# Fourier mixing with a gated convolution: the last 64 rows of two batches put into one tile of the last product

## The chip, the cores and the metric

The kernel runs on one core of a Trainium2 chip. The metric is the device time of one execution in microseconds (us). A difference of 2% or more would be called faster or slower.

## The reference, cut to what matters

```python
def _attn_ref(x):                       # x: 8 batches, 3136 rows, 256 features, fp32
    X = np.fft.fft(x, axis=1)
    X = np.fft.fft(X, axis=2)
    return X.real.astype(np.float32)

def _moe_ref(x, w_in, conv_w, w_out):   # w_in 256x1024, conv_w 3x1024, w_out 1024x256
    h = np.maximum(x @ w_in, 0.0)
    ...                                 # conv_out: three taps along the rows, zero at the ends of a batch
    gate = 1.0 / (1.0 + np.exp(-conv_out))
    return (h * gate @ w_out).astype(np.float32)
```

The real part of the transform is even in the rows, so the kernel computes half the rows and mirrors them. What matters here is the last product, `(h * gate) @ w_out`: its rows are cut into tiles of at most 128, and 3136 is 24.5 times 128.

## The kernel before

The kernel is one loop of 256 steps: 8 batches, 4 chunks of rows each, 8 blocks of 128 hidden features each. The stages of a step are spread over several turns of the loop, so that all engines work at once:

```python
    for t in range(n + LAG):            # LAG = 3
        ...
        sigmoid(steps[t - 2])           # ScalarE
        products(steps[t + 1])          # TensorE: pb and pa, the two halves of x @ w_in
        copies(steps[t + 1])            # ScalarE: nb
        combine(steps[t])               # VectorE: h, reads pa in PSUM and nb in SBUF
        run("dve")                      # VectorE: input folding or transform of a later batch
        first_tap(steps[t])             # ScalarE
        other_taps(steps[t - 1])        # VectorE: two taps
        gate(steps[t - 2])              # VectorE one half, GpSimd the other
        mm2(steps[t - LAG])             # TensorE: the last product
        run("pe")                       # TensorE: transform of the next batch
```

("..." marks cuts; conditions on `t` are left out.) A batch has 6, 6, 6 and 7 tiles in its four chunks. The seventh tile of the last chunk has 65 rows. Eight feature blocks times eight batches make 64 products of seven tiles. The gate is a multiplication of two tensors, cut in the middle:

```python
        m = n // 2
        gt(g[:, m:n], g[:, m:n], h[:, m + 1:n + 1], op=ALU.mult)     # GpSimd
        vt(g[:, 0:m], g[:, 0:m], h[:, 1:m + 1], op=ALU.mult)         # VectorE
```

The copies of finished tiles use three buffers of two tiles; a chunk of seven tiles needs four.

## Time and profile before

| | before |
|---|---|
| time, median of 3 runs | 1308.8 us (1307.44 to 1309.79) |
| span of the profiled execution | 1303.7 us |
| TensorE busy | 1203.4 us, 92% |
| VectorE busy | 1190.7 us, 91% |
| products of seven tiles | 64 |

Of the groups of instructions by shape, three (columns: line, engine, operation, output from inputs, shape, count, then busy us, mean ns of one, and idle time before them):

```profile
L514 POOL TENSOR_TENSOR g<-g,h 128x417 f32<-128x417 f32 x64 | 62.0, 969 | 217.4 <-ACT g L507 92.6 <-DVE h L492 58.8 <-issue 34.2
...
L174 DVE TENSOR_TENSOR w<-xh 99x508 f32<-99x508 f32 x16 | 16.6, 1040 | 0.0
...
L175 DVE TENSOR_TENSOR w<-xh 99x508 f32<-99x508 f32 x16 | 10.8, 676 | 0.0
```

L174 and L175 fold the input of a later batch on VectorE. They have the same shape and the same number of elements, one adds and one subtracts, and yet one takes 1040 ns and the other 676. L514 is GpSimd's half of the gate of a last chunk. The timeline of a step in the stretch of batch 3 shows how they stand to each other (columns: start us, duration us, engine, line, operation, then the wait before it in brackets):

```profile
695.22 0.59 DVE L515 TENSOR_TENSOR g<-g,h 128x416 f32<-128x416 f32 x1
...
695.72 1.09 DVE L492 CUSTOM_DVE_ANT_0 h<-pa,nb 128x418 f32<-128x418 f32 x2
...
696.37 0.92 POOL L514 TENSOR_TENSOR g<-g,h 128x417 f32<-128x417 f32 x1 [3.71 <-ACT g L507]
696.72 1.11 DVE L174 TENSOR_TENSOR w<-xh 99x508 f32<-99x508 f32 x1
...
697.75 0.67 DVE L175 TENSOR_TENSOR w<-xh 99x508 f32<-99x508 f32 x1
```

L492, which reads PSUM, runs beside GpSimd's half and takes its usual time (two instructions in 1.09 us; over the whole trace, those of 417 columns take 583 ns on average where they overlap GpSimd's half, 57 of them, and 582 where they do not, 7 of them). L174, which reads two tensors in SBUF, begins beside it at 696.72 and takes 1.11 us. L175, begun after GpSimd is done, takes 0.67. So 0.44 us of L174's "busy" time look like time in which VectorE does not advance.

### The profile page before, as it was taken

The numbers are of one execution on the slowest core, as the hardware profiler recorded it, in microseconds if no ns is written. First come the engines' busy times: TensorE is split into PE (matmuls) and PEld (weight loads), VectorE is DVE, ScalarE is ACT, GpSimd is POOL, SyncE is SP. The second block draws the span as 40 slices with busy tenths as digits, with TensorE's granted clock in tenths as the row PEclk, the third lists the DMA queues.
The fourth block names the chain that finished last, engine by engine and source line by source line (L and its number), as shares of the span: only waits on it lengthen the run. The fifth ranks groups of instructions, "written<-read, shape, count | busy, mean of one in ns | idle before, by whom it ended". The sixth has DMA issues, their size and how long they took to land.

```text
span 1303.7 us, 15202 instructions
## 1 busy us (share of the span) xinstructions
PE 1203.4 (92%) x4914; PEld 898.9 (69%) x4914; DVE 1190.7 (91%) x1664; ACT 857.4 (66%) x1558; POOL 406.7 (31%) x507
## 2 busy tenths in 40 slices
PE   0758999999999999999899999999999999999998
PEld 0525677777677766777677776777677777777776
DVE  6869999999999998999899998999989888898996
ACT  0226676666667666677667776766767777777885
POOL 2415434241523234232513225241322223122222
PEclk9968999999999999999999999999999999999999
DMA  7601203020211112020202103020010001000011
GB/s 227 185 25 45 80 25 99 1 77 25 88 36 49 49 29 74 25 77 25 72 29 62 39 25 94 30 76 1 25 50 25 27 25 42 20 14 27 25 33 43
DMA packets 46841, 66.02 MB, mean 51 GB/s; under 512 B 5601, under 2 KB 35197, under 8 KB 46505
## 3 DMA queue, kind: packets, MB, share of 16 engines
q1 hardware_dynamic: 41012, 49.80, 12.1%
q0 software_dynamic: 5120, 12.85, 3.4%
q10 hardware_dynamic: 628, 2.40, 0.6%
q8 instruction: 38, 0.62, 0.2%
q14 instruction: 43, 0.34, 0.1%
HBM read 39.24 MB, written 25.74 MB: 50 GB/s over the span
## 4 chain that ended last, share of the span: by engine, by line
PE 57%; DVE 26%; issue 8%; ACT 4%; POOL 2%; DMA 2%; DVEq 0%; POOLq 0%; ACTq 0%; SPq 0%
PE po L89 36%; PE pb L89 8%; DVE g L504 7%; PE pa L89 7%; PE pd L89 6%; DVE h L492 4%; DVE g L515 4%; ACT nb L481 2%; DVE w L174 2%; DVE w L175 1%; DVE xh L158 1%; DVE xh L147 1%; DVE xh L163 1%; POOL er L319 1%; DVE xh L162 1%
## 5 line engine op out<-in xcount | busy, mean ns | idle before, releaser
L89 PE MATMUL po<-wout,g 128*128 128x256 f32 (+2 forms) x3200 | 744.9, 383 | 37.4 <-DVE g L515 22.0
L89 PEld LDWEIGHTS po<-wout,g 128*128 128x128 f32 (+2 forms) x3200 | 598.6, 189 | 206.0 <-DVE g L515 59.2
L504 DVE SCALAR_TENSOR_TENSOR g<-h,cw,g 128x770 f32<-128x770 f32 (+2 forms) x512 | 579.9, 1133 | 10.9 <-ACT g L498 1.8
L514 POOL TENSOR_TENSOR g<-g,h 128x385 f32<-128x385 f32 (+1 forms) x256 | 240.5, 941 | 775.4 <-ACT g L507 434.7
L507 ACT ACTIVATE g<-g 128x770 f32<-128x770 f32 (+2 forms) x256 | 220.6, 862 | 253.3 <-DVE g L504 252.2
L481 ACT ACTIVATE nb<-pb 128x386 f32<-128x386 f32 (+4 forms) x512 | 225.8, 494 | 95.7 <-PE pb L89 94.0
L492 DVE CUSTOM_DVE_ANT_0 h<-pa,nb 128x386 f32<-128x386 f32 (+4 forms) x512 | 265.1, 559 | 14.6 <-PE pa L89 9.6
L498 ACT ACTIVATE g<-h,cw 128x770 f32<-128x770 f32 (+2 forms) x256 | 243.8, 952 | 0.7 <-DVE h L492 0.7
L89 PE MATMUL pa<-pt,G 128*128 128x386 f32 (+2 forms) x512 | 213.6, 498 | 9.1 <-ACT pa L466 9.1
L89 PE MATMUL pb<-qt,G 127*128 127x386 f32 (+2 forms) x512 | 215.7, 502 | 4.5 <-ACT nb L481 4.5
L466 ACT ACTIVATE pa<-eb,ge 128x386 f32<-128x386 f32 (+2 forms) x256 | 154.0, 602 | 8.1 <-DMA eb<-ed 8.1
L515 DVE TENSOR_TENSOR g<-g,h 128x385 f32<-128x385 f32 (+2 forms) x256 | 153.0, 598 | 4.2 <-ACT g L507 4.2
L89 PEld LDWEIGHTS pa<-pt,G 128*128 128x128 f32 x512 | 97.5, 191 | 83.6 <-issue 21.0
L89 PE MATMUL pd<-tab,w 99*128 99x196 f32 (+2 forms) x448 | 119.0, 375 | 0.0
L89 PEld LDWEIGHTS pb<-qt,G 127*128 127x128 f32 x512 | 94.3, 191 | 31.8 <-ACT nb L481 7.7
L122 POOL DMA_INDIRECT xh<-in_x_dram,idx x64 | 88.8, 1388 | 16.4 <-issue 12.8
L89 PEld LDWEIGHTS pd<-tab,w 99*128 99x128 f32 (+1 forms) x448 | 83.7, 191 | 13.7
L531 ACT COPY os<-po 128x256 f32<-128x256 f32 (+2 forms) x200 | 59.8, 393 | 17.1 <-DMA out_dram<-os 9.6
L158 DVE TENSOR_TENSOR xh<-xh 98x1024 f32<-98x1024 f32 (+1 forms) x32 | 46.6, 1460 | 0.1
L147 DVE TENSOR_TENSOR xh<-xh 98x1020 f32<-98x1020 f32 (+1 forms) x32 | 45.6, 1435 | 0.0
L89 PE MATMUL po<-win,dm 128*128 128x512 f32 x8 | 5.7, 879 | 38.4 <-DMA dm<-dft_dim_dram 38.4
L174 DVE TENSOR_TENSOR w<-xh 98x508 f32<-98x508 f32 (+1 forms) x32 | 31.1, 971 | 0.1
(84 smaller groups left out, 350.8 us busy)
## 6 DMA issues: line engine op xcount, KB each, us to landing
out_dram<-os SPq DMA_DIRECT2D x184, 128.0 KB
xh<-in_x_dram SPq DMA_DIRECT2D x16, 784.0 KB
eb<-ed SPq DMA_DIRECT2D x16, 193.0 KB
tab<-dft_seq_dram SPq DMA_DIRECT2D x4, 601.8 KB
raw<-in_moe_w_in_dram ACTq DMA_DIRECT2D x2, 1024.0 KB
raw<-in_moe_w_out_dram SPq DMA_DIRECT2D x1, 2048.0 KB
eb<-ed SPq DMA_DIRECT2D x8, 209.0 KB
eb<-ed SPq DMA_DIRECT2D x8, 192.5 KB
```

Of the source, the lines that this page charges most:

```text
L89: nc.tensor.matmul(o, l, r, start=start, stop=stop, skip_group_check=True)
L122: nc.gpsimd.indirect_dma_start(out=xh[b, h][0:NP, 4 + m].rearrange("p q d -> p (q d)"), out_offset=None, in_=bass.AP(tensor=x.tensor, offs ...
L158: vt(flat(to, to + 2), flat(0, 2), flat(2, 4), op=op)
L466: act(pa[s][:, 0:n], eb[b, c], AF.Copy, scale=ge[:, f:f + 1])
L481: act(nb[s][:, i, cols], p[:, cols], AF.Copy, scale=-1.0 if i else 1.0)
L492: nc.vector._custom_dve(TENSOR_ADD_SAT, out=to, in0=a[:, cols], in1=c[:, i, cols], s0=BIG, s1=0.0)
L498: act(gs[s], hs[s][:, 0:n], AF.Copy, scale=cw[:, 0, s[2]:s[2] + 1])
L504: stt(out=g, in0=h[:, k:k + n], scalar=cw[:, k, f:f + 1], in1=g, op0=ALU.mult, op1=ALU.add)
L507: act(gs[s], gs[s], AF.Sigmoid)
L514: gt(g[:, m:n], g[:, m:n], h[:, m + 1:n + 1], op=ALU.mult)
L515: vt(g[:, 0:m], g[:, 0:m], h[:, 1:m + 1], op=ALU.mult)
L531: nc.scalar.copy(out=osb[0:m, j % 2], in_=pt[0:m, j % 2])
```

## The change

Its intent is to stop spending a whole tile on 65 rows. The limits of the chunks are moved so that every tile has 128 rows and 64 rows are left over per batch. The left-over rows of an even and an odd batch share one tile, `left`, which stays in SBUF and is multiplied with the odd batch. So the last chunk of an even batch has six tiles, and that of an odd batch has seven. VectorE writes the left-over columns with a multiply of its own, 64 wide, and the gate of a last chunk is split into 384 and 384 columns in place of 416 and 417. The core of the diff (moves of buffers and the arithmetic of the chunk limits are cut):

```diff
+    left = const.tile([P, NF, P], F32, name="left")
 ...
     def gate(s):
+        b, c, f = s
         g, h = gs[s], hs.pop(s)
         n = g.shape[1]
+        if chunks[c].last:
+            o = chunks[c].rest[0]
+            vt(left[:, f, b % 2 * LEFT:(b % 2 + 1) * LEFT], g[:, o:n], h[:, o + 1:n + 1], op=ALU.mult)
+            n = o
         m = n // 2
 ...
     def mm2(s):
-        tiles = chunks[c].tiles
-        for i, (o, r, m) in enumerate(tiles):
+        ch = chunks[c]
+        tiles = [(gs[s][:, o:o + m], [(0, b, r, m)]) for o, r, m in ch.tiles]
+        if ch.last and b % 2:
+            tiles.append((left[:, f], [(i * LEFT, b - 1 + i, ch.rest[1], LEFT) for i in range(2)]))
+        for i, (w, to) in enumerate(tiles):
 ...
-                    nc.sync.dma_start(out=rows[b * S + r:b * S + r + m, :], in_=osb[0:m, j % 2])
+                    for p0, b_, r, m in tiles[j][1]:
+                        nc.sync.dma_start(out=rows[b_ * S + r:b_ * S + r + m, :], in_=osb[p0:p0 + m, j % 2])
```

Besides, to make room for `left`, the pool of transform copies becomes four equal buffers, and the pool of broadcasts loses one of its five; the fourth broadcast of a batch is loaded later.

More of the change, by code (lines that the diff above doesn't have):

```diff
@@ L69 @@
     erp = ctx.enter_context(tc.tile_pool(name="erp", bufs=1))
-    ebp = ctx.enter_context(tc.tile_pool(name="ebp", bufs=5))
-    asp = ctx.enter_context(tc.tile_pool(name="asp", bufs=2))
+    ebp = ctx.enter_context(tc.tile_pool(name="ebp", bufs=4))
+    asp = ctx.enter_context(tc.tile_pool(name="asp", bufs=4))
     pqp = ctx.enter_context(tc.tile_pool(name="pqp", bufs=2))
@@ L252, in copy @@
             def copy(p):
-                a_[sn, c] = asp.tile([P, HO], F32, name="as", tag="as")
+                a_[sn, c] = asp.tile([P, HO + 2], F32, name="as", tag="as")
                 nc.scalar.copy(out=a_[sn, c][:, 0:n], in_=p[:, 0:n])
@@ L271, in copy @@
             def copy(p):
-                a_[sn] = asp.tile([P, HO + QO], F32, name="as", tag="ao")
-                nc.scalar.copy(out=a_[sn][:, HO:], in_=p[:, 0:QO])
+                a_[sn], a_["e0"] = [asp.tile([P, HO + 2], F32, name="as", tag="as") for _ in range(2)]
+                nc.scalar.copy(out=a_["e0"][:, 0:QO], in_=p[:, 0:QO])
             def fin(p):
-                a, e0, e2 = a_[sn], a_[sn][:, HO:], p[:, QO:2 * QO]
+                a, e0, e2 = a_[sn], a_["e0"][:, 0:QO], p[:, QO:2 * QO]
                 vt(a[:, 0:QO], e0, e2, op=ALU.add)
@@ L305, in copy @@
             def copy(p):
-                a_["e"] = asp.tile([P, HO + QO], F32, name="as", tag="ao"), asp.tile([P, HO], F32, name="as", tag="as")
+                a_["e"] = [asp.tile([P, HO + 2], F32, name="as", tag="as") for _ in range(2)]
                 for c in range(2):
@@ L330, in units, with spread @@
         return begin, [odd_even(1), odd(1), even(1, 0), even(1, 1), feature(), odd_even(0), odd(0), even(0, 0), even(0, 1)], row
-    def spread(b):
-        for c, ch in enumerate(chunks):
+    def spread(b, cs):
+        for c in cs:
+            ch = chunks[c]
             eb[b, c] = ebp.tile([P, HN], F32, name="eb", tag="eb")[:, 0:ch.k1 - ch.k0]
@@ L344, in __init__ @@
             c0 = CUTS[c]
-            c1 = CUTS[c + 1] if c + 1 < len(CUTS) else NK
-            self.k0, self.k1 = max(c0 - 1, 0), min(c1 + 1, NK)
+            self.last = c + 1 == len(CUTS)
+            c1 = NK - 1 if self.last else CUTS[c + 1]
+            self.k0, self.k1 = max(c0 - 1, 0), min(c1 + 2, NK)
             n = self.k1 - self.k0
-            f0 = 1 if c0 == 0 else 0
-            self.front = slice(f0, f0 + n)
-            b0, b1 = (1 if c0 == 0 else 0), (n - 1 if c1 == NK else n)
-            self.cols = slice(b0, b1)
-            self.back = slice(f0 + n, f0 + n + b1 - b0)
-            self.zeros = c0 == 0
-            self.w = self.back.stop + (1 if c0 == 0 else 0)
-            if c1 == NK:
-                runs = [(0, c0, S - 2 * c0 + 1)]
-            else:
-                runs = [(0, c0, c1 - c0), (f0 + n, S - c1 + 1, c1 - max(c0, 1))]
-            self.tiles = [(g + i, r + i, min(P, l - i)) for g, r, l in runs for i in range(0, l, P)]
+            self.zeros = c0 == 0
+            f0 = 1 if self.zeros else 0
+            nf = c1 + 1 - self.k0
+            b0, b1 = max(c0, 1) - self.k0, n - 1 if self.last else n
+            self.fcols, self.cols = slice(0, nf), slice(b0, b1)
+            self.front = slice(f0, f0 + nf)
+            self.back = slice(f0 + nf, f0 + nf + b1 - b0)
+            self.w = self.back.stop + f0
+            if self.last:
+                runs = [(0, c0, S - 2 * c0)]
+            else:
+                runs = [(0, c0, c1 - c0), (f0 + nf, S - c1, c1 - c0)]
+            self.tiles = [(g + i, r + i, P) for g, r, l in runs for i in range(0, l - LEFT, P)]
+            self.rest = (runs[0][2] - LEFT, runs[0][1] + runs[0][2] - LEFT)
+    LEFT = P // 2
+    assert B % 2 == 0 and all(c % P == 0 for c in CUTS) and (S - 2 * CUTS[-1]) % P == LEFT
     chunks = [Chunk(c) for c in range(len(CUTS))]
@@ L479, in copies @@
         nb[s] = nbp.tile([P, 2, HN], F32, name="nb", tag="nb")
-        for i, cols in enumerate((slice(0, n), ch.cols)):
+        for i, cols in enumerate((ch.fcols, ch.cols)):
             act(nb[s][:, i, cols], p[:, cols], AF.Copy, scale=-1.0 if i else 1.0)
@@ L490, in combine @@
             nc.gpsimd.memset(h[:, 0:ch.w:ch.w - 1], 0.0)
-        for i, (to, cols) in enumerate(((h[:, ch.front], slice(0, n)), (h[:, ch.back][:, ::-1], ch.cols))):
+        for i, (to, cols) in enumerate(((h[:, ch.front], ch.fcols), (h[:, ch.back][:, ::-1], ch.cols))):
             nc.vector._custom_dve(TENSOR_ADD_SAT, out=to, in0=a[:, cols], in1=c[:, i, cols],
@@ L518, in mm2 @@
         b, c, f = s
-        tiles = chunks[c].tiles
-        for i, (o, r, m) in enumerate(tiles):
+        ch = chunks[c]
+        tiles = [(gs[s][:, o:o + m], [(0, b, r, m)]) for o, r, m in ch.tiles]
+        if ch.last and b % 2:
+            tiles.append((left[:, f], [(i * LEFT, b - 1 + i, ch.rest[1], LEFT) for i in range(2)]))
+        for i, (w, to) in enumerate(tiles):
             if f == 0 and i % 2 == 0:
@@ L523, in mm2 @@
             pt = po[b, c, i // 2]
-            mm(pt[0:m, i % 2, :], gs[s][:, o:o + m], wout[:, f, :],
-               f == 0 and i % 2 == 0, f == NF - 1)
+            mm(pt[:, i % 2, :], w, wout[:, f, :], f == 0 and i % 2 == 0, f == NF - 1)
             if f == NF - 1 and (i % 2 or i == len(tiles) - 1):
@@ L529, in mm2 @@
                 for j in range(i - i % 2, i + 1):
-                    _, r, m = tiles[j]
-                    nc.scalar.copy(out=osb[0:m, j % 2], in_=pt[0:m, j % 2])
-                    nc.sync.dma_start(out=rows[b * S + r:b * S + r + m, :], in_=osb[0:m, j % 2])
+                    nc.scalar.copy(out=osb[:, j % 2], in_=pt[:, j % 2])
+                    for p0, b_, r, m in tiles[j][1]:
+                        nc.sync.dma_start(out=rows[b_ * S + r:b_ * S + r + m, :], in_=osb[p0:p0 + m, j % 2])
         gs.pop(s)
@@ L549 @@
         if i == 4:
-            spread(0)
+            spread(0, range(len(chunks)))
         for g in late_w[i::len(us)]:
@@ L591 @@
             at(cs[i + 1], "dve", u.fin)
-        at(cs[-1] - 2, "load", lambda b=b: spread(b))
+        at(cs[-1] - 2, "load", lambda b=b: spread(b, range(len(chunks) - 1)))
+        at(per * b + 1, "load", lambda b=b: spread(b, [len(chunks) - 1]))
     LAG = 3
```

## The prediction

> **What bounds the kernel now.** I first read the busy shares of the page.
>
> ```profile
> PE 1203.4 (92%) x4914; PEld 898.9 (69%) x4914; DVE 1190.7 (91%) x1664; ACT 857.4 (66%) x1558; POOL 406.7 (31%) x507
> ```
>
> TensorE and VectorE are one per cent apart over 1303.7 us, so work taken from one alone need not show in the time. Next come the groups by shape (busy us, mean ns, idle before).
>
> ```profile
> L89 PE MATMUL po<-wout,g 128*128 128x256 f32 x2944 | 690.3, 383 | 37.4 <-DVE g L515 22.0 <-POOL g L514 14.9
> L492 DVE CUSTOM_DVE_ANT_0 h<-pa,nb 128x386 f32<-128x386 f32 x256 | 130.5, 552 | 5.0 <-POOL g L514 5.0
> L89 PE MATMUL po<-wout,g 128*65 128x256 f32 x128 | 38.1, 379 | 0.0
> L492 DVE CUSTOM_DVE_ANT_0 h<-pa,nb 128x418 f32<-128x418 f32 x64 | 37.5, 586 | 0.0
> ```
>
> A tile of 65 rows costs what one of 128 costs (379 against 383 ns), so the last tile of each batch is half wasted: this is what the change goes for. But the same product waits 22.0 us for VectorE's half of the gate (L515).
>
> The question is which engine rules where the seventh tile stands. Steps run (batch, chunk, feature block); the loop does the last product three steps late, so the eight products of seven tiles fall at chunk 3, blocks 4 to 7 of the current step and chunk 0, blocks 0 to 3 of the next batch. I cut these stretches out of the trace for batches 0 to 6 (columns: us, then busy us and instructions of each engine).
>
> ```profile
> core 0: us, PE busy (x) PEld busy (x) DVE busy (x) ACT busy (x) POOL busy (x), PEclk, DMA share, GB/s
> 223.14:257.13 33.99, 32.45 (x131) 23.56 (x131) 32.69 (x43) 22.22 (x38) 7.70 (x11) 1.00 0.09 29
> 684.59:717.79 33.20, 32.20 (x132) 23.63 (x132) 32.46 (x44) 22.66 (x40) 12.50 (x17) 1.00 0.20 61
> 838.01:871.22 33.21, 32.19 (x132) 23.63 (x132) 32.47 (x44) 22.66 (x40) 12.49 (x17) 1.00 0.20 61
> 1138.78:1170.17 31.39, 31.39 (x131) 23.87 (x131) 29.85 (x42) 23.86 (x41) 7.66 (x11) 1.00 0.08 26
> ```
>
> In batches 0, 3 and 4 VectorE is busy longer than TensorE in just these stretches, because it folds the input of a later batch there; only in batch 6, where no fold is left, is TensorE full (31.39 of 31.39) and VectorE not. The timeline of batch 4's stretch (start, duration, instructions merged, wait in brackets) shows how:
>
> ```profile
> 853.89 0.59 DVE L515 TENSOR_TENSOR g<-g,h 128x416 f32<-128x416 f32 x1
> 854.53 3.29 PE L89 MATMUL po<-wout,g 128*128 128x256 f32 x14 [0.55 <-DVE g L515]
> ...
> 863.13 0.59 DVE L515 TENSOR_TENSOR g<-g,h 128x416 f32<-128x416 f32 x1
> 863.77 3.29 PE L89 MATMUL po<-wout,g 128*128 128x256 f32 x14 [0.34 <-DVE g L515]
> ```
>
> TensorE's product begins the moment VectorE's gate ends. A shorter product would only wait longer.
>
> Last, the end of batch 6's stretch:
>
> ```profile
> 1171.47 3.18 PE L89 MATMUL po<-wout,g 128*128 128x256 f32 x14
> 1175.79 2.75 PE L89 MATMUL po<-wout,g 128*128 128x256 f32 x12
> 1177.74 0.37 ACT L531 COPY os<-po 65x256 f32<-65x256 f32 x1 [2.83 <-DMA out_dram<-os]
> 1178.89 0.56 DVE L515 TENSOR_TENSOR g<-g,h 128x384 f32<-128x384 f32 x1 [3.05 <-ACT g L507]
> 1179.66 0.91 PE L89 MATMUL pb<-qt,G 127*128 127x385 f32 x2 [1.12 <-ACT nb L481]
> ```
>
> The copy of the seventh tile needs a fourth output buffer of three, waits 2.83 us for an output to land, and holds up ScalarE, then VectorE 3.05 and TensorE 1.12 us.
>
> [...]the 14 matmul instructions of seven tiles take 3.18 us and the 12 of six 2.75, so a tile costs 0.43 us[...]the trace has 551 ns for the 384-wide gate[...].
>
> **The change, part by part.**
>
> *Removed from TensorE.* In batches 0, 2, 4, 6 the eight last-chunk products go from seven tiles to six: 32 x 0.43 = 13.8 us, 1.05% of the time. The odd batches keep seven, the last of them the shared one.
>
> *Added to VectorE.* Each last-chunk step gets a 64-wide multiply into the shared tile, 64 in all; its own gate shrinks from 416 to 384 columns. A column costs (586-552)/32 = 1.06 ns in the rows above. In the trace of batch 3 the 416-wide gate starts at 704.46 and the next VectorE instruction at 704.96: 0.50 us, of which 416 x 1.06 = 0.44, so 0.06 is fixed. The new multiply then takes 0.06 + 64 x 1.06 = 0.13, less 32 x 1.06 = 0.03: +0.10 us per step (taps of 832 instead of 833 change nothing), 0.8 us per batch, 6.4 in all, by these estimates. The first two of the eight fall before a place where VectorE waits for the transform anyway, so 0.6 counts.
>
> *Moved.* The products of chunks 0 to 2 are one column wider[...]; VectorE's chunk 0 is four columns wider per step, 0.3 us. Perhaps 0.6 us on the path. The pool of copies becomes four equal buffers in rotation; in the built program no steady-state copy gets a new late wait, only the prologue's, and these end before the first seed, which waits for a DMA until 88.09. The late load of the fourth broadcast is over a chunk early.
>
> *On the path.* Even batches with folds (0, 2, 4): I only gain what VectorE stood still for because the transform behind the product came late. In the trace these VectorE waits are about 0.4 us (batch 0), 0.44 + 0.5 (batch 2), 0.44 + 0.73 (batch 4): 2.5 us; against them 3 x 0.6 = 1.8. Net -0.7. Odd batches 1, 3, 5: seven tiles still, VectorE rules, +0.6 each: +1.8. Batch 6: 8 x 0.43 = 3.4 us saved, and the stall of the fourth output buffer (1.1 on TensorE) gone, but VectorE, back to back from 1149 to 1175, then sets the pace with 0.1 more per step: I take -3.6. Batch 7: a drain with seven tiles, in which TensorE waits 0.17 us for the last gates already: +0.6; and the last tile now leaves in two DMAs, which the queue issues some 0.47 us apart (7 in 3.26 us): +0.4. Wider chunks +0.6. Sum: -0.7 + 1.8 - 3.6 + 1.0 + 0.6 = -0.9 us.
>
> **Rivals.** (1) *TensorE is the bound, and all 13.8 us come off*: 1295 us. For it: TensorE is the busiest engine, and on the chain of waits PE has 57%. Against it: the windows above; six of seven stretches have an idle TensorE that waits for L515. (2) *VectorE is the bound everywhere[...]*[...]. For it: VectorE is gapless in the fold stretches. Against it: consecutive VectorE instructions overlap in the trace (0.50 us from start to start against 0.58 of duration), and batches 6 and 7 have no folds. (3) *The output-buffer stall also matters in batches 0, 2, 4*: ScalarE waits about 1 us there (9.6 us over all eight batches), but VectorE runs on at those places; up to 2 us more gain if I misread it: 1306.
>
> **Range and chances.** 1308.8 - 0.9 gives 1308. The two uncertain terms are the multiply (0.08 to 0.2 us per step on some 50 steps: -1 to +5) and batch 6 (-2 to -4.5); the fold stretches may give 3 us more if TensorE's lead carries over into the mixed stretches after them. Together with 1 us of scatter between runs: 1302 to 1314. To leave the 2% band the time would have to fall under 1283, more than all the removed work, or rise over 1335, four times the added work. So within 2%: 0.97; faster 0.015; slower 0.015.
>
> **What would show it.** TensorE's busy time falls by about 13 us while the span falls by about one; its idle time before the last product, waiting for VectorE's gate, grows by about 8 us, in the stretches of batches 0, 2 and 4. VectorE's busy time rises by some 6 us[...]. The stretch of batch 6 gets about 3 us shorter, and the 2.83 us wait for an output buffer is gone; those of batches 1, 3, 5 get half a microsecond longer. If instead the stretches of batches 0, 2 and 4 each shrink by some 3 us, VectorE did not rule there, and I am wrong by up to 1%.

## The result, and the profile after

| | before | changed |
|---|---|---|
| time, median (lowest to highest) | 1309.3 us (1307.44 to 1310.51), 4 runs | 1301.93 us (1299.8 to 1303.91), 4 runs |
| ratio of the times | | 0.9945 (0.9924 to 0.9965) |
| span of the profiled execution | 1303.7 us | 1300.7 us |
| TensorE busy | 1203.4 us | 1192.5 us |
| VectorE busy | 1190.7 us | 1189.9 us |

A ratio is the mean time of one kernel's runs over that of the other's of the same rounds, so it is not quite the ratio of the medians beside it. The time lies within 2% of the kernel before, at the lower edge of the predicted range of 1302 to 1314 us (1301.93 here, 1302.33 in e1): the change gave some 7 us, not 0.9.

The busy shares of the changed kernel:

```profile
PE 1192.5 (92%) x4850; PEld 893.0 (69%) x4850; DVE 1189.9 (91%) x1728; ACT 857.0 (66%) x1554; POOL 398.2 (31%) x507
```

Its groups by shape that answer to those shown before:

```profile
L89 PE MATMUL po<-wout,g 128*128 128x256 f32 x3072 | 717.2, 383 | 44.4 <-DVE g L529 29.1 <-POOL g L528 14.6
...
L528 POOL TENSOR_TENSOR g<-g,h 128x384 f32<-128x384 f32 x64 | 58.3, 912 | 219.7 <-ACT g L516 129.5 <-PE pa L89 29.9 <-issue 29.8
L546 ACT COPY os<-po 128x256 f32<-128x256 f32 x196 | 58.3, 393 | 11.5 <-PE po L89 8.1 <-DMA out_dram<-os 2.2 <-PE pb L89 1.2
...
L174 DVE TENSOR_TENSOR w<-xh 99x508 f32<-99x508 f32 x16 | 15.0, 940 | 0.0
L525 DVE TENSOR_TENSOR left<-g,h 128x64 f32<-128x64 f32 x64 | 14.7, 229 | 0.4 <-ACT g L516 0.4
...
L175 DVE TENSOR_TENSOR w<-xh 99x508 f32<-99x508 f32 x16 | 10.8, 676 | 0.0
```

TensorE lost 10.9 us of busy time, where about 13 were foretold, and waits 29.1 us for VectorE's gate where it waited 22.0. The copy of a seventh tile no longer waits 9.6 us for an output in all, as the group of 65-row copies did before; what is left is 2.2. The new multiply is there, 64 times 229 ns. But VectorE's busy time did not rise, and L174 fell from 1040 to 940 ns without being touched by the diff. These are the folds of 99 rows. Of those of 98 rows L174 rose from 901 to 974 ns and L175 fell from 763 to 675, so no single line shows the sum; it is worked out below.

The same stretches as in the prediction, cut at the same places of the program (batches 0, 3, 4 and 6; us, then busy us and instructions of each engine):

```profile
core 0: us, PE busy (x) PEld busy (x) DVE busy (x) ACT busy (x) POOL busy (x), PEclk, DMA share, GB/s
223.82:256.94 33.12, 29.49 (x117) 21.56 (x117) 32.19 (x50) 22.30 (x38) 6.17 (x10) 1.00 0.11 35
686.11:719.21 33.10, 32.22 (x131) 24.30 (x131) 32.47 (x52) 22.74 (x40) 12.24 (x17) 1.00 0.23 68
838.42:870.63 32.21, 29.48 (x117) 21.50 (x117) 31.58 (x51) 22.72 (x40) 11.53 (x17) 1.00 0.23 69
1138.76:1167.48 28.72, 28.65 (x117) 21.67 (x117) 27.70 (x45) 22.84 (x40) 6.85 (x10) 1.00 0.13 36
```

In the even batches 0 and 4 TensorE is now busy 29.5 us of 33.1 and 32.2, so most of what it no longer does became idle time. Batch 6 is 2.67 us shorter and TensorE is still full there (28.65 of 28.72). Batch 3, which still has seven tiles and has eight more VectorE instructions (52 against 44), is 0.1 us shorter, where the prediction had it half a microsecond longer.

To see all batches I laid the start times of VectorE's steps side by side (the start of `combine`, L492 before and L501 after). A row is the time from the start of step (batch, chunk 3, block 2) to that of (next batch, chunk 0, block 7): thirteen steps, which hold all eight gates and all eight last products of a last chunk. Batch 7 has no successor, so its end is taken on its own: from the end of TensorE's last product to the end of the span.

| stretch | before | changed | changed, second trace (e1) |
|---|---|---|---|
| batch 0 | 62.18 | 61.42 | 61.38 |
| batch 1 | 61.43 | 61.20 | 61.18 |
| batch 2 | 60.84 | 60.53 | 60.53 |
| batch 3 | 60.84 | 60.75 | 60.72 |
| batch 4 | 60.87 | 60.51 | 60.52 |
| batch 5 | 58.44 | 58.34 | 58.32 |
| batch 6 | 55.94 | 51.50 | 51.47 |
| sum of the seven | 420.54 | 414.25 | 414.12 |
| after the last product | 3.9 | 5.3 | 5.3 |

The stretches give 6.3 us, and the end takes 1.4 back. Two thirds of the gain is batch 6. Outside the stretches the two traces differ by one to two microseconds either way, for which the clock is the likely cause: after some pauses of 1.9 to 2.95 us in TensorE's work, the records show its granted clock at half for 3.4 or 6.8 us, and not at the same places in each execution (after 200 us, and but for the last 20, at 793.4 and 947.0 us in the trace of before, 3.4 us each; at 639.8, for 6.8 us, and 947.0, for 3.4, in that of the changed kernel). Between the stretches of batches 2 and 3, for example, the changed kernel's trace has 6.8 us at half clock and takes 93.9 us; that of before has none there and takes 91.8. Times over several runs average over this, a single trace does not.

The same kind of step as shown for before, in the changed kernel, at almost the same time:

```profile
696.72 0.22 DVE L525 TENSOR_TENSOR left<-g,h 128x64 f32<-128x64 f32 x1
...
696.85 0.56 DVE L529 TENSOR_TENSOR g<-g,h 128x384 f32<-128x384 f32 x1
697.32 1.09 DVE L501 CUSTOM_DVE_ANT_0 h<-pa,nb 128x418 f32<-128x418 f32 x2
...
697.87 0.86 POOL L528 TENSOR_TENSOR g<-g,h 128x384 f32<-128x384 f32 x1 [3.76 <-ACT g L516]
698.32 0.95 DVE L174 TENSOR_TENSOR w<-xh 99x508 f32<-99x508 f32 x1
```

The multiply moves the gate by 0.13 us, from 696.72 to 696.85, and the gate then takes 0.47 to the next instruction, against 0.50 before: together 0.10 more, as predicted. But L174, which now starts later relative to GpSimd's half, takes 0.95 instead of 1.11. It gives back 0.16 us, more than the 0.10. This is what the experiments had to explain.

The end of the program, first in the kernel before and then in the changed one (the last product, the stores merged into one line, the last copy):

```profile
1294.38 5.34 PE L89 MATMUL po<-wout,g 128*128 128x256 f32 x24
...
1298.00 3.26 SPq L532 DMA_DIRECT2D out_dram<-os  x7
...
1300.30 0.37 ACT L531 COPY os<-po 65x256 f32<-65x256 f32 x1 [0.32 <-DMA out_dram<-os]
```

```profile
1293.61 4.49 SPq L548 DMA_DIRECT2D out_dram<-os  x8
...
1294.74 0.59 PE L89 MATMUL po<-wout,left 128*128 128x256 f32 x2
...
1295.92 0.37 ACT L546 COPY os<-po 128x256 f32<-128x256 f32 x1 [0.33 <-DMA out_dram<-os]
```

TensorE is done at 1299.72 (1294.38 + 5.34) before and at 1295.33 (1294.74 + 0.59) after. The span ends 3.9 us (at 1303.66) and 5.3 us (at 1300.66) later. Eight stores are issued instead of seven, because the last tile goes to two batches, and issuing takes 4.49 us instead of 3.26.

### The profile page after: what moved, and what is told of

It is laid out like the page before. It is cut to its first block, busy times and chain, and to the rows that moved or that the text cites. A ratio compares the mean times of both kernels' runs of the same rounds, so it can differ in the third digit from the quotient of the medians. Undisturbed runs are those within 1.5% of the kernel's fastest.

```text
span 1300.7 us, 15302 instructions
## 1 busy us (share of the span) xinstructions
PE 1192.5 (92%) x4850; PEld 893.0 (69%) x4850; DVE 1189.9 (91%) x1728; ACT 857.0 (66%) x1554; POOL 398.2 (31%) x507
## 4 chain that ended last, share of the span: by engine, by line
PE 55%; DVE 28%; issue 8%; ACT 4%; POOL 2%; DMA 2%; DVEq 0%; POOLq 0%; SPq 0%; ACTq 0%
PE po L89 33%; PE pb L89 9%; DVE g L513 8%; PE pa L89 7%; PE pd L89 6%; DVE h L501 5%; DVE g L529 4%; ACT nb L490 2%; DVE w L174 1%; DVE xh L147 1%; DVE xh L158 1%; DVE w L175 1%; DVE xh L163 1%; POOL er L319 1%; DVE xh L162 1%
## 5 line engine op out<-in xcount | busy, mean ns | idle before, releaser
L89 PE MATMUL po<-wout,g 128*128 128x256 f32 x3072 | 717.2, 383 | 44.4 <-DVE g L529 29.1
L89 PEld LDWEIGHTS po<-wout,g 128*128 128x128 f32 x3072 | 578.8, 190 | 209.6 <-DVE g L529 75.8
L513 DVE SCALAR_TENSOR_TENSOR g<-h,cw,g 128x770 f32<-128x770 f32 (+1 forms) x512 | 574.4, 1122 | 10.3 <-ACT g L507 1.2
L516 ACT ACTIVATE g<-g 128x770 f32<-128x770 f32 (+1 forms) x256 | 220.5, 861 | 256.8 <-DVE g L513 256.5
L490 ACT ACTIVATE nb<-pb 128x386 f32<-128x386 f32 (+3 forms) x512 | 225.8, 494 | 93.1 <-PE pb L89 91.3
L501 DVE CUSTOM_DVE_ANT_0 h<-pa,nb 128x386 f32<-128x386 f32 (+3 forms) x512 | 265.3, 560 | 15.9 <-PE pa L89 9.0
L507 ACT ACTIVATE g<-h,cw 128x770 f32<-128x770 f32 (+1 forms) x256 | 243.2, 950 | 0.8 <-DVE h L501 0.8
L89 PE MATMUL pa<-pt,G 128*128 128x387 f32 (+2 forms) x512 | 214.8, 500 | 7.2 <-ACT pa L475 7.2
L89 PE MATMUL pb<-qt,G 127*128 127x387 f32 (+2 forms) x512 | 217.4, 506 | 3.5 <-ACT nb L490 3.5
L475 ACT ACTIVATE pa<-eb,ge 128x387 f32<-128x387 f32 (+2 forms) x256 | 154.2, 602 | 7.7 <-DMA eb<-ed 7.5
L174 DVE TENSOR_TENSOR w<-xh 98x508 f32<-98x508 f32 (+1 forms) x32 | 30.6, 957 | 0.1
```

The lines of the kernel that those rows point to most:

```text
L89: nc.tensor.matmul(o, l, r, start=start, stop=stop, skip_group_check=True)
L475: act(pa[s][:, 0:n], eb[b, c], AF.Copy, scale=ge[:, f:f + 1])
L490: act(nb[s][:, i, cols], p[:, cols], AF.Copy, scale=-1.0 if i else 1.0)
L501: nc.vector._custom_dve(TENSOR_ADD_SAT, out=to, in0=a[:, cols], in1=c[:, i, cols], s0=BIG, s1=0.0)
L507: act(gs[s], hs[s][:, 0:n], AF.Copy, scale=cw[:, 0, s[2]:s[2] + 1])
L513: stt(out=g, in0=h[:, k:k + n], scalar=cw[:, k, f:f + 1], in1=g, op0=ALU.mult, op1=ALU.add)
```

## The experiments

Two theories stood at the start. **The clash**: GpSimd's half of the gate slows VectorE's next instruction that reads two SBUF operands (in the step of before, L174 took 1.11 us beside it and L175 0.67 after it); the multiply pushes that instruction out of its way and the smaller half ends sooner, so the multiply is free. **The tiles alone**: the gain is only removed tiles and the removed wait for an output buffer, and the multiply costs its 0.10 us. The "before" is 1308.75 us for e1 to e4, 1308.54 for e5 to e8, 1307.69 for e9 to e11 and 1307.68 for e12. All outputs are right.

### e1: the changed kernel again

No edit.

> The changed kernel itself once more, for a tighter size. Its first four runs gave 0.9945 of the kernel before; the two profiles, laid side by side, give 4.4 us gained by the end of the work and 1.4 lost again in the last outputs, with a jitter of 1 to 2 us where TensorE's clock drops after the stall in chunk 2 of some batches. I expect a ratio of 0.994 to 0.996. If the ratio is nearer 0.998, the 3.0 us between the two profiles is the true size and the runs of the first session were lucky.

Measured: 1302.33 us (1301.08 to 1305.01), ratio 0.9953 (0.994 to 0.9966). The gain of 6 to 7 us is real, and the stretches of the second trace agree with the first within 0.04 us.

### e2: seven tiles in every batch

```diff
-        if ch.last and b % 2:
-            tiles.append((left[:, f], [(i * LEFT, b - 1 + i, ch.rest[1], LEFT) for i in range(2)]))
+        if ch.last:
+            tiles.append((left[:, f], [(b % 2 * LEFT, b, ch.rest[1], LEFT)]))
 ...
+    nc.gpsimd.memset(left[:, :, LEFT:P], 0.0)
```

(The memset runs once, so that batch 0 reads no unset memory.) Everything of the change but its purpose: the shared tile is multiplied in every batch, and each batch stores its own 64 rows.

> The changed kernel with its TensorE saving undone: the shared tile is multiplied in the even batches too, and only the 64 rows of that batch are written, so there are 50 products again and the fourth output buffer is needed again; chunk limits, widths and the 64-wide multiply stay. My theory (VectorE rules the stretches of batches 0, 2, 4; TensorE only that of batch 6): about 4.4 us come back in the stretch from batch 6 to 7 and about 0.4 us in each of batches 0, 2, 4, so 5 to 6 us slower than the changed kernel, no more than 1 us from the kernel before. Rival (TensorE is the bound everywhere): all 13.8 us come back, so it would be slower than the kernel before by some 6 us.

Measured: 1306.97 us, ratio 0.9981 (0.9968 to 0.9994). So the 32 removed tiles are worth 4.6 us (1306.97 against 1302.33), of 13.8 us of TensorE work. This is not quite the tiles alone: the seventh tile also brings back the fourth output buffer (ScalarE's copies wait 7.4 us for outputs in all, 2.2 in the changed kernel), and the end has one store less. In the stretches the difference is 0.6 in batch 0, 0.2 in batches 2 and 4 each, and 2.7 in batch 6 (54.18 to 51.50), where 4.4 were expected. The rest of the change, with 64 more instructions on VectorE, is not slower than before but 1.8 us faster, more than the 1 us that was expected at most. The moved buffers and the wider chunks are inside these 1.8 us; they were not tested alone.

### e3: an output buffer for the seventh tile, in the kernel before

```diff
+    osl = ctx.enter_context(tc.tile_pool(name="osl", bufs=1))
 ...
-                osb = osp.tile([P, 2, D], F32, name="os", tag="os")
+                if i == 6:
+                    osb = osl.tile([P, 1, D], F32, name="ol", tag="ol")
+                else:
+                    osb = osp.tile([P, 2, D], F32, name="os", tag="os")
```

> The kernel before with an output buffer of its own for the seventh tile of a batch, and nothing else. Theory: only the stall from batch 6 to 7 was on the path, 1.3 us of TensorE's idle time there, so 1.1 to 1.5 us faster than the kernel before; the waits in the other batches vanish without effect. Rival 3 of the prediction: they matter too, and it gains 3 us or more.

Measured: 1307.27 us (1306.79 to 1312.39), ratio 0.9995 (0.9979 to 1.001). In total this is inconclusive, because one run of the six was high and the interval holds 1. In the trace it is clear: the stretch of batch 6 goes from 55.94 to 53.28, and those of batches 0, 2 and 4 stay at 62.00, 60.85 and 60.83. The output wait costs time only in batch 6. How much is better read from TensorE, because VectorE takes 1.3 of the 2.7 us longer again in batch 7. TensorE's step in which the wait stands, from the start of its product `pb` to that of the next step, goes from 5.17 to 3.89 us and the step after it from 3.99 to 3.89: 1.4 us, as expected. The wait's size varies, too: the same step took 4.77 us in e4, which has the same buffers, and 3.89 in e2, where ScalarE waits only 0.90 us.

### e4: only GpSimd's half made smaller, in the kernel before

```diff
-        m = n // 2
+        m = n - 384 if n == 833 else n // 2
```

VectorE takes 449 of 833 columns in a last chunk, so GpSimd has 384 as in the changed kernel. VectorE does more, nothing is removed.

> The kernel before, with the gate of the last chunk cut at 449 instead of 416, so that GpSimd has 384 columns as in the changed kernel and VectorE 33 more. Prediction's accounting (each column of VectorE counts): 0.035 us more per step of VectorE, 64 steps, so 0 to 2 us slower, and the stretches of batches 1, 3, 5 get 0.2 us longer. New theory (VectorE's next instruction with two operands in SBUF is slowed while GpSimd's half of the gate runs; a longer VectorE gate and a shorter GpSimd gate let them miss each other): the overlap shrinks by 0.06 + 0.035 us, so VectorE gains about 0.06 us net per step: the stretches of batches 1, 3, 5 get 0.3 to 0.5 us shorter, VectorE's busy time falls by 3 to 4 us, the whole is 1 to 3 us faster.

Measured: 1306.32 us, ratio 0.9979 (0.9966 to 0.9992). Thirty-three columns more per step on VectorE, one of the two busiest engines, and the kernel is faster by some 2 us. L174 fell from 1040 to 985 ns. The stretches of batches 1, 3 and 5 shrank by 0.32, 0.21 and 0.24 us and VectorE's busy time by 2.2 us, a little less than the new theory expected (0.3 to 0.5 and 3 to 4), but in its direction and against the other. This speaks for the clash and against the tiles alone.

### e5: the new multiply done twice

```diff
             vt(left[:, f, b % 2 * LEFT:(b % 2 + 1) * LEFT], g[:, o:n], h[:, o + 1:n + 1], op=ALU.mult)
+            vt(dup, g[:, o:n], h[:, o + 1:n + 1], op=ALU.mult)
```

> The changed kernel, with the 64-wide multiply done once more per last-chunk step into a scratch tile nobody reads. Prediction's accounting: 0.13 us per step counts where VectorE rules, some 48 steps, so 5 to 6 us slower than the changed kernel, VectorE's busy time 8 us up. New theory: the slowdown of VectorE's next two-operand instruction beside GpSimd's gate, still about 0.27 us per step in the changed kernel (0.95 against 0.68 us for one of the input-folding instructions), shrinks by the same 0.13, so the step keeps its length: within 1.5 us of the changed kernel, VectorE's busy time up by less than 3 us.

Measured: 1300.61 us (1299.58 to 1304.31), ratio 0.9945 (0.9931 to 0.9959), against 0.9953 for the changed kernel: the same. A second multiply of the same size was free here. Its timeline in the stretch of batch 3:

```profile
694.79 0.22 DVE L526 TENSOR_TENSOR left<-g,h 128x64 f32<-128x64 f32 x1
...
694.92 0.22 DVE L528 TENSOR_TENSOR dup<-g,h 128x64 f32<-128x64 f32 x1
695.06 0.55 DVE L532 TENSOR_TENSOR g<-g,h 128x384 f32<-128x384 f32 x1
...
695.93 0.86 POOL L531 TENSOR_TENSOR g<-g,h 128x384 f32<-128x384 f32 x1 [3.75 <-ACT g L517]
696.53 0.81 DVE L174 TENSOR_TENSOR w<-xh 99x508 f32<-99x508 f32 x1
```

The second multiply costs 0.14 us more from start to start (694.92 to 695.06), and L174 takes 0.81 in place of 0.95: 0.14 less.

### e6: the multiply four times, three of them into one scratch tile

As e5 with `for _ in range(3)`.

> The changed kernel, with the 64-wide multiply done three more times per last-chunk step. Added work 0.39 us per step. Prediction's accounting: some 48 steps x 0.39 = 19 us slower than the changed kernel, and more in the last two batches. New theory: the first 0.27 us are paid by the vanishing slowdown, the rest is not: about 0.12 us per step, 5 to 8 us slower. If both extra runs are slower in proportion to the added instructions, the new theory falls.

Measured: 1323.51 us, ratio 1.0108 (1.0091 to 1.0124). Now it costs, 21 us above the changed kernel: as a number this is nearer to the prediction's accounting (19) than to the new theory (5 to 8). The doses were not as planned, though. The three write the same tile, and here a multiply behind another of the same tile starts 0.25 to 0.26 us after it instead of 0.13 to 0.14; the three take 0.65 us together. E9 repeats the test with the planned dose. A step of this run:

```profile
707.48 0.74 DVE L528 TENSOR_TENSOR dup<-g,h 128x64 f32<-128x64 f32 x3
708.13 0.55 DVE L532 TENSOR_TENSOR g<-g,h 128x384 f32<-128x384 f32 x1
708.49 0.92 POOL L531 TENSOR_TENSOR g<-g,h 128x384 f32<-128x384 f32 x1 [3.87 <-PE pa L89]
...
709.60 0.68 DVE L174 TENSOR_TENSOR w<-xh 99x508 f32<-99x508 f32 x1
```

GpSimd's half ends at 709.41, before L174 starts at 709.60, and L174 takes its free 0.68 us. There is nothing left to give back.

### e7: 64 columns of every gate from GpSimd to VectorE, in the changed kernel

```diff
-        m = n // 2
+        m = n // 2 + 64
```

> The changed kernel, with 64 columns of every gate moved from GpSimd to VectorE in all chunks (449 and 321 of 770). Prediction's accounting: VectorE gets 0.068 us more per step on 256 steps, most of it on the path: 5 to 15 us slower. New theory: GpSimd's half gets 0.12 us shorter (1.8 ns a column) and VectorE's next instruction starts 0.07 us later, so up to 0.19 us of slowdown per step goes for 0.07 us of work: VectorE's busy time falls by 15 to 30 us, and the whole gets 5 to 15 us faster, until TensorE rules (its busy time, 1192 us, does not change). This would be a kernel that beats both.

Measured: 1295.28 us, ratio 0.99 (0.9885 to 0.9915). This gives VectorE 64 columns more in each of 256 steps, 17.4 us of work at 1.06 ns a column, and the kernel is 7 us faster than the changed one. VectorE's busy time falls from 1189.9 to 1179.0, by 10.9 us where 15 to 30 were expected.

### e8: the last of the eight stores on ScalarE's queue

```diff
-                        nc.sync.dma_start(out=rows[...], in_=osb[p0:p0 + m, j % 2])
+                        eng = nc.scalar if b == B - 1 and p0 else nc.sync
+                        eng.dma_start(out=rows[...], in_=osb[p0:p0 + m, j % 2])
```

> The changed kernel, in which the second of the last batch's two half-tile stores is issued from ScalarE's queue. In the profiles the time from TensorE's last product to the end is 5.4 us in the changed kernel and 4.0 in the one before; the last store is issued 0.56 us after the one before it. Theory: the second store costs this; issued beside the first, it brings back 0.5 to 1.2 us, to be seen in that tail. Rival: the tail is a round trip that either store takes, and nothing changes.

Measured: 1300.91 us, ratio 0.9935 (0.9922 to 0.9949). In the total, 0.6 us is too little to tell. In the traces the time from the end of TensorE's last product to the end is 3.9 us before, 5.3 changed, 4.8 here, and 4.5 in e2, which stores only 64 rows there. So the second store costs about 0.8 us of the 1.4, and a second queue gives back half a microsecond of it; where the other 0.6 comes from stays open. Each of these is one trace; in the other runs with both stores on one queue the end took 5.2 to 6.1 us.

### e9: three extra multiplies that do not wait for each other

As e6, but each writes a third of the scratch tile, `dup[:, i]`, so that they add about 3 times 0.13 us.

> The four-fold multiply again, mended: in the run before, the three extra ones wrote one tile, so each waited for the one ahead (0.22 us each instead of 0.13) and the step got 0.66 us longer before its gate, not 0.39. Here each writes a tile of its own. New theory: of 3 x 0.13 = 0.39 us per step, 0.27 are paid by the slowdown that vanishes beside GpSimd's half of the gate, about 0.12 is left: 8 steps x 7 stretches x 0.12 = 5 to 8 us slower than the changed kernel (1307 to 1310), VectorE's busy time 7 to 9 us up for 25 us of added work. Prediction's accounting (each counts): 48 steps x 0.39 = 19 us slower, 1320 or more.

Measured: 1310.61 us (1308.73 to 1316.62), ratio 1.0029 (1.0007 to 1.005): 8.3 us above the changed kernel by the medians and 9.9 by the ratios, just above the 5 to 8 that were expected, and far from 19. VectorE's busy time is 10.5 us up, where 7 to 9 were expected. The seven stretches sum to 421.36 us, 7.2 more than in e1; over 56 steps this is 0.13 each, of 0.39 added. So about 0.26 us per step is absorbed, and what goes beyond costs its full length.

### e10: 96 columns of every gate to VectorE, in the changed kernel

As e7 with `n // 2 + 96`.

> The changed kernel with 96 columns of each gate moved to VectorE instead of 64. With 64 the time fell to 1295.3 and the input-folding instruction beside GpSimd's gate took 0.78 us, 0.10 over its free 0.68. 32 columns more cost VectorE 0.034 us and shift the two by 0.034 + 0.06. Theory: the rest of the slowdown goes, and the gain per step is 0.06 at most where it was still there: 1290 to 1296, level with or a little better than 64 columns. Rival (only the move of columns off GpSimd matters): another 3 us, 1292 or less. If the knee is passed it is slower than with 64.

Measured: 1295.29 us, ratio 0.99 (0.9885 to 0.9914), the same as 64.

### e11: 64 columns to VectorE, in the kernel before

The edit of e7, without the change.

> The kernel before the change, with 64 columns of every gate moved from GpSimd to VectorE. If this gain has nothing to do with the change, it is as large here as on the changed kernel: 1301.5 to 1304 (7 us less than before), and VectorE's busy time falls by some 12 us. If the gain needs TensorE's shorter products (TensorE is the bound again once VectorE is relieved), it is less than 4 us.

Measured: 1302.2 us, ratio 0.9955 (0.994 to 0.9969). The shift of the gate is worth as much alone as the whole change; both together (e7) give about the sum.

### e12: 80 columns, and the last store on ScalarE's queue

The edits of e8 and of e7, with `n // 2 + 80`.

> The two gains together: the changed kernel with 80 columns of each gate moved to VectorE (64 and 96 both gave 1295.3) and the last batch's second half-tile store on ScalarE's queue (0.6 us of tail in the run with it alone). Both at work: 1294 to 1295.5, a ratio of 0.989 to 0.991. If the optimum of the split lies between the two by more than a flat top, 1293 or less.

Measured: 1291.53 us (1288.87 to 1292.65), ratio 0.9872 (0.9855 to 0.989). It is the fastest kernel, 1.3% under before and some 0.8% under the changed kernel, and it beat what was expected by 2.5 us. By its expectation, a time under 1293 would mean that the best split lies between 64 and 96; the traces do not show that. Compared with e7, its seven stretches are 1.6 us shorter (407.10 against 408.67), and its end after the last product is shorter as well. Compared with e10 the stretches are the same (407.14), so part of the 3.8 us by which the medians differ stays open. GpSimd's half and the fold in it:

```profile
L528 POOL TENSOR_TENSOR g<-g,h 128x304 f32<-128x304 f32 x64 | 49.9, 779 | 225.1 <-ACT g L516 135.8 <-issue 29.8 <-PE pa L89 26.0
...
L174 DVE TENSOR_TENSOR w<-xh 99x508 f32<-99x508 f32 x16 | 11.9, 744 | 0.0
```

### What the traces say together

The expectations above speak of GpSimd "slowing" VectorE. Read again with all traces at hand, the matter is stricter than that: a VectorE instruction with two SBUF operands that starts while GpSimd's half runs ends a fixed time after the end of that half, to a few nanoseconds. For the four steps shown:

| step shown | GpSimd's half ends | L174 starts | takes | ends after GpSimd's end |
|---|---|---|---|---|
| before | 697.29 | 696.72 | 1.11 | 0.54 |
| changed | 698.73 | 698.32 | 0.95 | 0.54 |
| e5, one extra | 696.79 | 696.53 | 0.81 | 0.55 |
| e6, three extra in a row | 709.41 | 709.60 | 0.68 | starts after it, not held |

The end of L174 is tied to GpSimd's end, wherever it starts. Over the whole trace of before, 181 VectorE instructions with two SBUF operands start while GpSimd's half runs. All but three of them end a fixed time after it, which their width sets: the 21 folds of 508 elements 539 to 543 ns (the middle four fifths), the 50 taps of 770 columns 815 to 819, the 18 folds of 1024 elements 1077 to 1080. That is 1.04 ns per column and 12 to 15 ns. If the two ran side by side, each slower, those that start later would end later. They do not: it is as if VectorE's instruction stood still until GpSimd's half is done. The other way round it is the same: 11 of the 64 last-chunk halves of GpSimd start inside such a VectorE instruction; the 8 of them that start 98 ns or more after it end 0.78 us after its end, and take 1.15 to 1.68 us in place of 0.92. The other three start 23 to 27 ns after it and take their 0.93 us, and the VectorE instruction ends 0.83 us after them. What reads PSUM is not held, as L492 above: that of 386 columns takes 550 ns where it overlaps GpSimd's half (105 times) and 552 where it does not (151). What makes the two wait for each other the traces do not show.

So VectorE has a wait in such a step that no view calls a wait: the profile books it as busy time of the held instruction. I summed what these instructions take beyond their free duration (1.04 ns per column, and 147 ns for a plain multiply or add, which gives L175's 676, or 214 for a tap, which gives 1015 for 770 columns, where the median is 1021), for each trace:

| kernel | hidden wait, us | VectorE busy, us | time, us |
|---|---|---|---|
| before | 75.6 | 1190.7 | 1308.8 |
| e4, last chunks' half 384 | 70.1 | 1188.5 | 1306.3 |
| changed | 68.3 | 1189.9 | 1302.3 |
| e5, one extra multiply | 64.2 | 1190.7 | 1300.6 |
| e9, three apart | 57.4 | 1200.4 | 1310.6 |
| e6, three in a row | 56.2 | 1210.2 | 1323.5 |
| e7, 64 columns moved | 41.3 | 1179.0 | 1295.3 |
| e12, 80 columns and store | 35.9 | 1175.9 | 1291.5 |
| e10, 96 columns moved | 30.4 | 1175.7 | 1295.3 |

From before to changed, the multiply adds 64 times 0.10 us, 6.4, and the hidden wait falls by 7.3. VectorE's busy time should then fall by 0.9; it falls by 0.8, from 1190.7 to 1189.9. From the changed kernel to e7, 17.4 us of work come to VectorE and 27.0 of waiting go. From e12 to e10, 16 columns more cost VectorE 16 x 1.06 ns x 256 = 4.3 us of work and save 5.5 of waiting, so the curve is nearly flat there.

## Why the prediction was right or wrong

**What rules where: right.** Removing TensorE's work in the stretches of batches 0, 2 and 4 mostly made TensorE wait longer for VectorE's gate, 29.1 us against 22.0, where about 8 more were foretold. Rival 1, that all 13.8 us come off, is excluded: e2 puts the removed products at 4.6 us. The fold stretches of even batches gained 1.4 us together (0.76, 0.31 and 0.36), where -0.7 was foretold.

**The cost of the multiply: right in size, wrong in effect.** This is the step that failed: "+0.10 us per step", of which "0.6 counts" per batch and "+0.6 each" falls on the odd batches, and with it "VectorE's busy time rises by some 6 us". The 0.10 is what the trace has (0.13 + 0.47 against 0.50). But it does not reach the path. In these steps the next VectorE instruction with two SBUF operands waits for GpSimd's half anyway, and that half, 0.06 us shorter in the steps shown (0.92 to 0.86), sets when it ends. So such a step gets about 0.06 shorter instead of 0.10 longer. Not every step is of this kind: the stretches of batches 1, 3 and 5 went down by 0.23, 0.09 and 0.10 us, 0.4 together, against +1.8 foretold. E5 and e9 show it by dose: the first 0.26 us added per step was free, the rest was not. E4 shows the other side: the smaller half alone makes the kernel faster. The prediction looked at VectorE as an engine without pauses, because it took busy time for work; L174 at 1040 ns beside L175 at 676 was in the profile and was not asked about. Rival 2, with VectorE as the bound everywhere, erred the same way: with the multiply at its measured 229 ns, less 0.03 for the 32 columns that the gate lost, it would have been 64 x 0.20, some 13 us more on VectorE, and VectorE's busy time fell by 0.8.

**Batch 6: right, too small.** Foretold -3.6, measured -4.4 (55.94 to 51.50). The terms are the same, less the 0.1 per step for the multiply, which again was not there. TensorE's steps split it, each from the start of its `pb` to the next: the output wait gives 1.4 us (before against e3; 1.1 foretold, and it changes from run to run), and the eight removed tiles give 3.1 (the nine steps that hold them take 39.6 us in e3 and in e2, 36.5 in the changed kernel; 3.4 foretold).

**Rival 3, the output wait in other batches: excluded.** With a buffer of its own (e3) the stretches of batches 0, 2 and 4 changed by 0.2 us or less.

**The end: right in sign, mis-sized.** Foretold +0.6 for the drain of batch 7 and +0.4 for the two stores. Measured +1.4 after TensorE's last product, so outside the drain, which took only 0.1 us longer (34.62 to 34.71, from the start of step (batch 7, chunk 3, block 2) to the end of the last product). The issue of a further store was counted at 0.47 us; against e2, with everything behind it, it costs about 0.8.

**Wider chunks, +0.6: not seen.** The 0.6 was the author's estimate, and no run has the wider chunks alone. Outside the stretches single traces differ by one to two microseconds, likely through the clock (after 200 us, and but for the last 20, the trace of before has 6.8 us at half clock and that of the changed kernel 10.2), so 0.6 could not show there.

**The sum.** The terms as measured are -1.4 - 0.4 - 4.4 + 1.4 = -4.8 us, where -0.9 was foretold. The second trace of the changed kernel is just that much shorter than the trace of before (1298.9 against 1303.7). The medians differ by 6.4 to 7.4. The remaining 1.6 to 2.6 us stay open. The profiled executions are not the middle ones: that of before took 1305.44 us, 3.4 less than the median of its runs, and that of e1 1301.09, 1.2 less than its median. Outside the stretches the granted clock falls to half at places that differ between executions (639.8 us in the changed kernel, 793.4 before), and I could not tie the rest to a part of the change. That the time still fell at the edge of the range is in part luck: the range allowed for a larger gain in batch 6, in the fold stretches and by scatter, not for a multiply that costs nothing.

## What to carry to other kernels

Before you charge a new instruction to a busy engine, look whether its neighbours of one shape have different durations: here L174, 1040 ns on average with GpSimd's half often beside it, where L175 took 676, had a wait in disguise, and what was added ahead of it was free until that wait was used up (0.26 us per step, e9). Where VectorE and GpSimd shared the gate, the even split was not the best one, because GpSimd's end held VectorE up (68.3 us in the changed kernel, 41.3 in e7): moving 64 to 96 of some 385 columns to the busier engine gained about half a percent. Work taken from an engine is worth only what it does in the stretches where that engine rules; here a third of 13.8 us.

## What this case measured of the hardware

- The time in which a VectorE instruction is held by GpSimd's half is inside its duration and counts as busy (some 76 of VectorE's 1190.7 us, by the sum above). The held instruction ends 12 to 15 ns plus its columns at about 1.04 ns after the other's end (815 to 819 ns for 50 taps of 770 columns), where one that runs free takes 147 or 214 ns plus its columns; why is not shown.
- Work ahead of a held instruction was free up to a point: 0.26 us per step was absorbed (e9), and one extra multiply of 64 columns in 64 steps did not lengthen the kernel (ratio 0.9945 with it, 0.9953 without).
- Multiplies of 64 columns into separate tiles start 0.13 to 0.14 us apart (e5, e9), and into the same tile 0.25 to 0.26 us apart (e6).
- Half clock came after pauses of TensorE of two to three microseconds, but not after all of them: between 200 us and the last 20 us, the 14 traces have 63 pauses of 1.86 to 2.95 us, of which 39 were followed within 4 us by 3.4 or 6.8 us at half clock, and no half clock came without one; in those of before and the changed kernel it is 10 pauses, 4 of them followed so. In the changed kernel's trace the pause of 2.66 us at 637.8 us was, and the one of 2.67 us at 488.5 was not.
- A store more at the end of the program: with the last tile in two stores of 64 rows the end came 5.3 us after the last product, with one store of 64 rows 4.5 (e2).
